# An xLSTM-style attention and two feed-forward layers on one core: queries and keys split in place instead of by a trip through DRAM, and a new order of work

## The chip, the cores and the metric

The kernel runs as one program on 1 core of a Trainium2 chip. The metric is the device time of one execution in microseconds (us), as a median of several runs; lower is better. Engines are named as in the profile: PE is TensorE (PEld its weight loads), DVE is VectorE, ACT is ScalarE, POOL is GpSimd, SP is SyncE, which issues all DMAs of this kernel, one after the other.

## The reference

Three layers follow each other. The attention is a recurrence over 768 steps for 4 batches of 8 heads with a head size of 40:

```
m_new  = maximum(f_gate[t] + m, i_gate[t])
f_stab = exp(f_gate[t] + m - m_new)
i_stab = exp(i_gate[t] - m_new);  m = m_new
C = f_stab * C + i_stab * outer(v[t], k[t])
n = f_stab * n + i_stab * k[t]
y[t] = sigmoid(o_gate[t]) * (C @ q[t]) / maximum(abs(n . q[t]), 1)
```

Its output, as 3072 rows of 320, goes through `maximum(maximum(x @ w1, x @ w2), x @ w3) @ w_out` (320 to 768 to 320; FFN1 below) and then through `h = x @ w_in; g = h * clip(h + 3, 0, 6) / 6; g @ w_out` (320 to 2048 to 320; FFN2 below). All weights are handed over as float64.

## The kernel before

The attention is cut into chunks of 128 steps. A group g is one batch in one chunk, so there are 24 groups, g = 4 * chunk + batch; `attention(g)` adds all steps of one. In a group, `scan` (L502) builds the decay matrix `fd` of each head on DVE, `sc` (L530) multiplies keys by queries on PE, `p` (L538) multiplies the scores by the decays, `inter` (L558) multiplies queries by the state of the chunk before, `pv` (L600) multiplies by the values, `rr`, `y0` and `y1` normalize, `tr` and `x` (L653, L658) transpose the result into `x1`, the input of FFN1, and `dc`, `cn` (L681, L700) carry the state on.

A product that has to keep nearly float32 accuracy is made of products in float32r: a number is split into a rounded high part and the remaining low part, and high*high, low*high and high*low are summed. For groups 8 to 23 (`GF = 8`) the three stand below each other on 120 rows of one tile: `qs` [120, 2, 8, 128] holds queries (index 0) and keys (index 1), and rows 0-39, 40-79 and 80-119 hold such parts that one product over 120 rows sums all three. Groups 0 to 7 use plain float32.

How `qs` of a group comes about, before: `lq` (L427) loads queries and keys as [128, 640] (`raw`), `sq` (L453, ACT) rounds them into the high part, `sl` (L457, POOL) subtracts for the low part, `sw` (L463) writes both parts to `qs_d` in DRAM (640 KB), and `sr` (L468) reads them back in five DMAs into the rows where they are wanted (960 KB):

```
nc.sync.dma_start(q[0:D], d[0].rearrange("a d n -> d a n"))
for r, (zq, zk) in enumerate(((0, 1), (1, 0)), 1):
    nc.sync.dma_start(q[r * D:r * D + D, 0], d[zq, 0])
    nc.sync.dma_start(q[r * D:r * D + D, 1], d[zk, 1])
```

The state of a group is spread over 120 rows (`cs`) in the same way: `ch` (L707, ACT) rounds, `cl` (L711, POOL) subtracts, `cd` (L716) moves the parts with six DMAs.

Weights are converted from float64 by steps on three engines, 24 pieces for FFN1 (`weights`, L732) and 32 for FFN2 (`w2_prep`, L939): a load (`load_f64`, L246, tile `raw`, four buffers), two conversions on ACT (`rebase` L251, `tail` L259), a join on DVE (L266), a rounding on ACT and a subtraction on POOL or DVE (`split`, L273). ACT reads a piece from its buffer, so a load can only go out when ACT is done with the piece four loads earlier.

FFN1 runs over blocks of 2, 2, 4, 4, 4, 4 and 4 groups (`BLK1`) and 6 pieces of 128 hidden columns: `f_in` (L773) makes three times eight matmuls into PSUM tile `h` (two buffers), whose first result is copied by ACT (`m`, L785) and the others joined by DVE (L787); `hh` (ACT, L797) and `hl` (POOL, L801) split the maximum, `f_out` (L806) multiplies it by the output weights into `acc`. `xd` (L850) writes the result to DRAM, two DMAs for each group; `x_load` (L952) reads it back for FFN2, which runs over 6 blocks of 512 rows and 16 pieces (`g_in` L971, `g_out` L991).

The order of the attention and of FFN1 on every engine is fixed before the program is built: each step is added with an engine, an assumed cost in ns, a priority (`pr`), the tiles it reads and writes; `Plan.order` (L143) plays them through with these costs and the buffer counts of `BUFS`, always takes the step that can start first (by priority where several can), and the instructions are written out in that order. `MOVED` (L42) adds a number to the priority of single steps. Priorities are 1000 * g plus an offset in `attention`, `WP0 + WPR * n` for the weights; `AHEAD` (L37) is how many groups ahead a group's queries may be loaded, `GP` and `NSG` place the gates of the chunks 1 to 5. FFN2 is ordered by the framework's own scheduler, which also puts its first weight loads and conversions among the steps of the attention. An engine works through its instructions strictly in the order written, SP as well: where one waits, all behind it wait.

Of the kernel before, what the change touches and what calls it, by code (L numbers as in the profile page):

```python
# [36 lines left out]
AHEAD, WP0, WPR = 5, 500, 100  # L37
GP, NSG = 1900, 4
GPB, GGB = 3, 4
PE_, PM, PC = 0, 2 * 10**6, 3 * 10**6  # L40

MOVED = {  # L42
    135: -1449, 206: -3641, 217: -1367, 319: 149, 371: 268, 387: 4201, 480: 39, 517: 2678, 522: 1135,
    539: 1040, 553: -4154, 559: -4352, 565: -156, 594: 613, 659: -1758, 707: -7, 715: 420, 742: -3344,
    940: 2702, 941: 5996, 953: 4436,
# [1035 lines left out]
```

## Time and profile before

| | |
|---|---|
| median of 3 runs | 793.09 us (789.65 to 795.54) |
| the profiled execution: time | 792.57 us |
| its span | 790.8 us |
| mean granted PE clock | 0.956 of full |
| PE busy | 757.2 us (96%), 5063 matmuls |
| DVE busy | 400.6 us (51%), 618 instructions |
| ACT busy | 309.2 us (39%), 597 instructions |
| POOL busy | 423.3 us (54%), 388 instructions |
| DMA, share of 16 engines | 38.2%, 91.82 MB |

The profile shows one execution; its span runs from the first to the last instruction, and 1.8 us of the time lie outside of it. Busy shares are means over a program with different stages: attention and FFN1 together in the first 380 us or so, the rest of FFN1 until 440 us, FFN2 until the end. The clock of PE is granted at one of two levels, 2.4 GHz (1.00 in the rows) or 1.2 GHz (0.50); a mean between them says how much of a stretch was spent at each.

### The profile page before, as it was taken

Reading aid. Unit: us, or ns where it says so; the run is one execution under the profiler, and the core shown is the slowest. Engines: PE = TensorE matmul, PEld = TensorE weight load, DVE = VectorE, ACT = ScalarE, POOL = GpSimd, SP = SyncE. Lnnn points to the kernel's source line nnn. Section 1 sums busy time; section 2 is a strip of 40 time slices with the busy share of each in tenths; the row PEclk is TensorE's granted clock in tenths of the full one; section 3 lists DMA queues with packets and bytes.
Section 4 is the critical chain, followed back from the end, with each engine's and each line's share of the span. In section 5 each row is a group of like instructions: output and inputs, shape, how many; then the busy total and the mean of one; then the engine's idle time right before and its main releaser. Section 6 shows DMA issues by size and latency. Waiting matters only on the chain.

```text
span 790.8 us, 13152 instructions
## 1 busy us (share of the span) xinstructions
PE 757.2 (96%) x5063; PEld 661.8 (84%) x5063; DVE 400.6 (51%) x618; ACT 309.2 (39%) x597; POOL 423.3 (54%) x388
## 2 busy tenths in 40 slices
PE   8878969899999998999999999999999999999997
PEld 6768869788888787888888878898998899898986
DVE  5987738668868776578425665312212113121210
ACT  4585422222223122222415886634433334433432
POOL 3788737757768687573514456535334334333331
PEclk7689679999999999999999999999999999999999
DMA  8578567675657758743322642200100000000000
GB/s 260 164 242 273 162 170 200 161 239 178 199 175 212 228 158 246 233 148 84 112 59 76 202 157 72 68 1 10 59 1 0 34 1 1 34 1 1 34 1 34
DMA packets 52078, 92.65 MB, mean 117 GB/s; under 512 B 6032, under 2 KB 28528, under 8 KB 52016
## 3 DMA queue, kind: packets, MB, share of 16 engines
q1 hardware_dynamic: 52016, 91.82, 38.2%
q8 instruction: 40, 0.66, 0.3%
q14 instruction: 22, 0.18, 0.1%
HBM read 70.78 MB, written 18.43 MB: 113 GB/s over the span
## 4 chain that ended last, share of the span: by engine, by line
PE 60%; DMA 11%; ACT 5%; DVE 4%; POOL 4%; SPq 3%; issue 2%; POOLq 0%; ACTq 0%; DVEq 0%
PE pi L284 20%; PE h L284 13%; PE po L1003 6%; PE po L1002 6%; PE po L1004 6%; DMA qs<-qs_d 4%; PE acc L817 3%; DMA raw<-in_w 2%; DMA qs_d<-sp 2%; SPq L720 2%; DVE t L267 2%; PE sc L536 1%; DMA fd<-f_d 1%; ACT a L255 1%; PE acc L819 1%
## 5 line engine op out<-in xcount | busy, mean ns | idle before, releaser
L284 PE MATMUL h<-x,w 128*128 128x512 f32 (+1 forms) x1008 | 224.8, 374 | 6.7 <-ACT m L785 6.7
L988 POOL TENSOR_TENSOR gg<-r,gg 128x512 fp32r<-128x512 f32 x96 | 125.6, 1318 | 184.4 <-ACT gg L987 174.3
L284 PEld LDWEIGHTS h<-x,w 128*128 128x128 f32 x1008 | 175.7, 198 | 36.3 <-ACT m L785 8.1
L284 PE MATMUL pi<-xs,w 128*128 128x512 f32 x768 | 193.0, 395 | 1.5 <-ACT w L946 0.8
L985 DVE SCALAR_TENSOR_TENSOR r<-r,pi 128x512 f32<-128x512 f32 x96 | 64.3, 686 | 230.3 <-ACT r L984 230.1
L284 PEld LDWEIGHTS pi<-xs,w 128*128 128x128 f32 x768 | 140.8, 188 | 29.7 <-ACT w L946 1.1
L1002 PE MATMUL po<-w,gg 128*128 128x320 f32 x384 | 118.3, 310 | 1.1 <-ACT gg L987 0.5
L1003 PE MATMUL po<-w,gg 128*128 128x320 f32 x384 | 118.0, 309 | 0.0
L984 ACT ACTIVATE r<-pi,b 128x512 f32<-128x512 f32 x96 | 64.0, 687 | 133.8 <-PE pi L284 133.2
L1004 PE MATMUL po<-w,gg 128*128 128x320 f32 x384 | 111.2, 309 | 0.0
L801 POOL TENSOR_TENSOR hh<-m,hh 128x512 fp32r<-128x512 f32 (+1 forms) x42 | 51.1, 1216 | 70.2 <-ACT hh L797 68.9
L787 DVE TENSOR_TENSOR m<-h,m 128x512 f32<-128x512 f32 (+1 forms) x84 | 50.9, 606 | 63.6 <-PE h L284 51.2
L1002 PEld LDWEIGHTS po<-w,gg 128*128 128x128 f32 x384 | 72.1, 188 | 5.7 <-ACT gg L987 1.5
L817 PE MATMUL acc<-hh,w 128*128 128x512 f32 (+1 forms) x252 | 76.5, 382 | 0.0
L1003 PEld LDWEIGHTS po<-w,gg 128*128 128x128 f32 x384 | 72.1, 188 | 3.0
L987 ACT CAST gg<-r 128x512 fp32r<-128x512 f32 x96 | 59.0, 621 | 36.6 <-DVE r L985 34.4
L797 ACT CAST hh<-m 128x512 fp32r<-128x512 f32 (+1 forms) x42 | 23.5, 559 | 125.7 <-PE acc L817 117.2
L1004 PEld LDWEIGHTS po<-w,gg 128*128 128x128 f32 x384 | 70.4, 188 | 1.0 <-POOL gg L988 0.2
L274 POOL TENSOR_TENSOR w<-t,w 128x384 fp32r<-128x384 f32 (+2 forms) x46 | 49.0, 1073 | 22.0 <-ACT w L946 11.5
L506 DVE TENSOR_TENSOR_SCAN fd<-fd,ident 128x512 f32<-128x512 f32 x40 | 58.1, 1462 | 2.5 <-DMA fd<-f_d 2.5
L267 DVE SCALAR_TENSOR_TENSOR t<-a,t 128x384 uint32<-128x384 uint32 (+1 forms) x56 | 46.0, 840 | 15.6 <-ACT t L263 14.0
L817 PEld LDWEIGHTS acc<-hh,w 128*128 128x128 f32 x252 | 47.0, 200 | 6.3
(107 smaller groups left out, 971.9 us busy)
## 6 DMA issues: line engine op xcount, KB each, us to landing
raw<-in_w SPq DMA_DIRECT2D x34, 384.0 KB
kvo<-in_kvo SPq DMA_DIRECT2D x22, 488.0 KB
fd<-f_d SPq DMA_DIRECT2D x20, 512.0 KB
qs_d<-sp SPq DMA_DIRECT2D x16, 640.0 KB
qs<-qs_d SPq DMA_DIRECT2D x64, 160.0 KB
raw<-in_w SPq DMA_DIRECT2D x22, 320.0 KB
raw<-in_qkf SPq DMA_DIRECT2D x16, 320.0 KB
qs<-qs_d SPq DMA_DIRECT2D x16, 320.0 KB
```

The source lines that it names most:

```text
L267: nc.vector.scalar_tensor_tensor(out=t, in0=a.bitcast(U32), scalar=3, in1=t, op0=ALU.logical_shift_left, op1=ALU.bitwise_or)
L284: nc.tensor.matmul(ps, wt[:, a:a + 128], x[:, r], start=n == 0, stop=n == len(order) - 1)
L506: nc.vector.tensor_tensor_scan(out=half, data0=s.get(("bc", a), half), data1=ident4.rearrange("p h t -> p (h t)"), initial=0.0, op0=ALU.mu ...
L801: nc.gpsimd.tensor_tensor(out=t[:, 1], in0=T["m", j, k], in1=t[:, 0].bitcast(F32), op=ALU.subtract)
L817: nc.tensor.matmul(acc[a], wo[:, a * 128:128 + a * 128], h, start=first, stop=last)
L984: nc.scalar.activation(r, ps, AF.Relu, bias=b3)
L985: nc.vector.scalar_tensor_tensor(out=r, in0=r, scalar=6.0, in1=ps, op0=ALU.min, op1=ALU.mult)
L987: nc.scalar.copy(gg[:, 0], r)
L988: nc.gpsimd.tensor_tensor(out=gg[:, 1], in0=r, in1=gg[:, 0].bitcast(F32), op=ALU.subtract)
L1002: nc.tensor.matmul(po[t], hi, wo[:, 0:320], start=first, stop=False)
L1003: nc.tensor.matmul(po[t], hi, wo[:, 320:640], start=False, stop=False)
L1004: nc.tensor.matmul(po[t], lo, wo[:, 0:320], start=False, stop=last)
```

## The change

Queries and keys of the groups 8 to 23 are loaded three times from the input as float32, each time into 40 of 120 rows of a tile `raw`, queries (a = 0) and keys (a = 1) apart. A constant `lows` [120, 2] is 1 on the rows where the low part is wanted and 0 elsewhere. `hm` on ACT writes float32r(lows * raw) into `sp`, `ls` subtracts it from `raw` into `qs`: on rows with 0 that leaves the rounded number itself, on rows with 1 the low part. Both run in halves of four heads (z), `ls` on DVE for the queries and on POOL for the keys. The DRAM tiles `qs_d` and the steps `sq`, `sl`, `sw`, `sr` are gone.

```diff
-                    s["raw"] = sb("raw", g, [128, QF])
-                    nc.sync.dma_start(s["raw"], qkf[g - GF])
+                    s["raw", a] = q = sb("raw", f"{g}_{a}", [120, H, L])
+                    for r in range(3):
+                        nc.sync.dma_start(q[r * D:r * D + D].rearrange("p h t -> p (h t)"), qkf[g - GF, :, a])
...
+                def hm(a, z):
+                    s["sp", a, z] = sb("sp", f"{g}_{a}{z}", [120, 4, L], F32R)
+                    x = s["raw", a][:, 4 * z:4 * z + 4]
+                    nc.scalar.activation(s["sp", a, z], x, AF.Copy, scale=lows[:, a:a + 1])
+
+                def ls(a, z):
...
+                    eng = nc.gpsimd if a else nc.vector
+                    eng.tensor_tensor(out=s["qs"][:, a, x], in0=s["raw", a][:, x], in1=s["sp", a, z].bitcast(F32), op=ALU.subtract)
...
-                P.add("ACT", 760, pr - 3000, sq, r=[("raw", g)], w=[("sp", g)])
-                P.add("POOL", 2000, pr - 3000, sl, r=[("raw", g)], w=[("sp", g)])
-                P.add("SP", 60, pr - 3000, sw, r=[("sp", g)], w=[("qd", g)], size=8 * 128 * QF)
-                P.add("SP", 300, pr - 2500, sr, r=[("qd", g)], w=[QS], size=120 * 8192)
```

The state goes to its 120 rows differently: `ch` on ACT makes three roundings of half a state each, one of them straight to other rows; `cl` on POOL writes the low part straight into rows 0-39 of `cs`, in two halves; two DMAs instead of six copy the high part to rows 40-119.

```diff
-                for n, x in enumerate(("cl", "ch", "ch")):
-                    for r in range(2):
-                        nc.sync.dma_start(
-                            t[n * D:n * D + D, 4 * r:4 * r + 4].bitcast(F32), s[x][64 * r:64 * r + D].bitcast(F32)
-                        )
+                for r in (D, 2 * D):
+                    nc.sync.dma_start(cs()[r:r + D].bitcast(F32), s["ch"][0:D].bitcast(F32))
```

The tiles `x2_d` between FFN1 and FFN2 are one for each block of FFN2, so `xd` and `x_load` need two DMAs for a block instead of two for a group. The planner's numbers change too: buffers, costs of SP's steps (60 ns becomes 360 for a DMA), the assumed latency of a DMA, a few constants, and the table of moved priorities, which grows from 21 entries to 175. New source lines shift by about 16 (L248 is L264 after, L255 L271, L263 L279, L720 L736).

```diff
-AHEAD, WP0, WPR = 5, 500, 100
-GP, NSG = 1900, 4
+AHEAD, WP0, WPR = 6, 500, 100
+GP, NSG = 1055, 4
...
+WLP, QLP = 800, 4000
...
-    135: -1449, 206: -3641, 217: -1367, 319: 149, 371: 268, 387: 4201, 480: 39, 517: 2678, 522: 1135,
...
+    21: -933, 44: 4396, 52: -6654, 63: -799, 66: 12937, 73: -3105, 74: 2861, 88: 693, 95: -1749,
...
-    qs=2, raw=1, sp=1, kvo=2, kvg=2, fd=2, vt=2, vw=2, nm=2, rr=2, y=2, sg=2, ct=1, cn=B + 1, ch=1, cl=1, cs=B + 1,
+    qs=2, raw=2, sp=1, kvo=2, kvg=2, fd=2, vt=2, vw=2, nm=2, rr=2, y=2, sg=2, ct=1, cn=B, ch=1, cs=B,
...
-                end = dma + 2000
+                end = dma + 2500
```

Two places of the new order matter below. The first is SP around the first weight loads of FFN2 (`raw2_k_p` is piece k, part p of FFN2's weights, `raw1_5_3` the last of FFN1's, the digit after another name is the group). Before:

```order
L248 DMA raw2_0_1_5219<-in_w2 128x320
L720 DMA cs5_1139<-cl5_1131 40x168 x2
L720 DMA cs5_1139<-ch5_1113 40x168 x4
L498 DMA fd7_1162<-f0_d_72 128x1024
L438 DMA kvo8_1196<-in_kvo 128x976
L471 DMA qs8_1218<-qs_d8_73 40x2x1024
L473 DMA qs8_1218<-qs_d8_73 40x1024
L474 DMA qs8_1218<-qs_d8_73 40x1024
L473 DMA qs8_1218<-qs_d8_73 40x1024
L474 DMA qs8_1218<-qs_d8_73 40x1024
L248 DMA raw2_1_0_5244<-in_w2 128x384
L248 DMA raw2_1_1_5254<-in_w2 128x320
```

and after:

```order
L264 DMA raw1_5_3_969<-in_w1 128x320
L506 DMA fd6_982<-f0_d_72 128x1024
L456 DMA kvo6_1015<-in_kvo 128x976
L264 DMA raw2_0_0_5268<-in_w2 128x384
L264 DMA raw2_0_1_5278<-in_w2 128x320
L456 DMA kvo8_1120<-in_kvo 128x976
L264 DMA raw2_1_0_5303<-in_w2 128x384
L264 DMA raw2_1_1_5313<-in_w2 128x320
L447 DMA qs7_1145<-in_qk0 40x1024 x2
L736 DMA cs5_1132<-ch5_1127 40x336 x2
```

Before, nine rows of SP stand between `raw2_0_1` and `raw2_1_0`, among them six DMAs of the state and five reads of `qs`; after, only the load of `kvo8` does, and the state comes behind the weights. ACT has the conversions of these pieces (`a2_1_0`) in its order at about the same place. Before:

```order
L263 ACTIVATE t2_0_1_5223<-raw2_0_1_5219 128x320
L255 ACTIVATE a2_1_0_5246<-raw2_1_0_5244 128x384
L255 ACTIVATE a2_1_1_5256<-raw2_1_1_5254 128x320
L797 CAST hh1_0_1288<-m1_0_1133 128x256
L785 COPY m0_5_1303<-h0_5_0_1279 128x256
```

The second place is ACT among the groups 10 to 12, where the roundings `hm` (L474) are new. After:

```order
L474 ACTIVATE sp10_01_1825<-raw10_0_1591,lows_90 120x512
L474 ACTIVATE sp10_11_1844<-raw10_1_1637,lows_90 120x512
L474 ACTIVATE sp10_10_1875<-raw10_1_1637,lows_90 120x512
L813 CAST hh1_5_1900<-m1_5_1676 128x256
L474 ACTIVATE sp12_11_1907<-raw12_1_1846,lows_90 120x512
L801 COPY m2_1_1915<-h2_1_0_1889 128x512
L670 CAST x13_1929<-tr8_1910 128x3x128
L474 ACTIVATE sp11_01_1961<-raw11_0_1902,lows_90 120x512
L474 ACTIVATE sp11_00_2016<-raw11_0_1902,lows_90 120x512
L813 CAST hh2_0_2059<-m2_0_1810 128x512
```

Before, ACT has one row `sp` for a whole group; after there are four, often one right behind the other, in front of the copies `m` and `hh` of FFN1 on the same engine.

## Rows read from the trace of the kernel before

**Rows 1.** Busy time by stretch: us, each engine busy (count), PEclk, DMA share, GB/s

```profile
20.00:40.00 20.00, 17.37 (x108) 14.88 (x108) 18.09 (x28) 11.81 (x25) 14.48 (x15) 0.61 0.55 164
40.00:60.00 20.00, 15.27 (x137) 13.63 (x136) 16.88 (x30) 17.00 (x43) 16.43 (x19) 0.83 0.75 240
60.00:80.00 20.00, 17.28 (x168) 16.06 (x164) 15.02 (x28) 9.87 (x24) 16.53 (x19) 0.91 0.81 271
80.00:100.00 20.00, 18.22 (x144) 17.64 (x141) 14.49 (x26) 8.20 (x20) 15.06 (x16) 0.67 0.58 163
100.00:120.00 20.00, 13.89 (x108) 13.21 (x107) 7.58 (x16) 4.18 (x10) 7.59 (x9) 0.73 0.58 159
120.00:140.00 20.00, 20.00 (x205) 19.77 (x205) 15.29 (x30) 5.47 (x14) 15.14 (x17) 0.91 0.77 219
140.00:160.00 20.00, 17.94 (x171) 15.60 (x170) 14.95 (x24) 4.17 (x9) 14.76 (x16) 0.96 0.62 158
...
180.00:260.00 80.00, 80.00 (x679) 67.41 (x678) 63.27 (x98) 20.50 (x39) 60.43 (x59) 1.00 0.60 185
...
300.00:340.00 40.00, 37.45 (x281) 31.03 (x280) 23.72 (x39) 10.10 (x19) 23.56 (x23) 1.00 0.77 237
...
380.00:440.00 60.00, 60.00 (x268) 49.37 (x266) 28.30 (x35) 26.34 (x51) 22.98 (x17) 1.00 0.33 92
440.00:500.00 60.00, 57.45 (x306) 49.71 (x305) 36.04 (x51) 47.45 (x101) 33.11 (x27) 1.00 0.40 131
500.00:780.00 280.00, 280.00 (x1551) 252.11 (x1550) 60.45 (x83) 110.50 (x182) 110.02 (x82) 1.00 0.05 17
```

**Rows 2.** Timeline of ACT, 84 to 114 us: start, us, instruction [idle before, releaser]

```profile
105.91 0.54 ACT L255 ACTIVATE a<-raw 128x384 f32<-128x384 f32 x1 [12.27 <-DMA raw<-in_w]
```

**Rows 3.** Timeline of PE, 96 to 112 us

```profile
107.83 2.08 PE L284 MATMUL h<-x,w 128*128 128x256 f32 x8 [6.11 <-ACT m L785]
```

**Rows 4.** Timeline of SP, 70 to 108 us: time of issue, us to issue

```profile
85.45 1.54 SPq L720 DMA_DIRECT2D cs<-cl  x2
87.04 3.87 SPq L720 DMA_DIRECT2D cs<-ch  x4
91.03 0.41 SPq L498 DMA_DIRECT2D fd<-f_d  x1
91.55 0.36 SPq L438 DMA_DIRECT2D kvo<-in_kvo  x1
...
94.05 5.50 SPq L248 DMA_DIRECT2D raw<-in_w  x4
```

**Rows 5.** Waits of PE, whole span: who for what, us, times, longest

```profile
PE sc L536 <- DMA cs<-ch: 2.2, 1, 2.2
PE sc L536 <- DMA qs<-qs_d: 2.1, 1, 2.1
```

**Rows 6.** Groups by line and form: count, busy us, mean ns, idle before

```profile
L458 POOL TENSOR_TENSOR sp<-raw,sp 128x640 fp32r<-128x640 f32 x16 | 29.1, 1822 | 7.1 <-ACT sp L455 7.0
...
L593 DVE TENSOR_TENSOR pr<-fd 128x512 f32<-128x512 f32 x32 | 26.4, 838 | 0.5
...
L598 POOL TENSOR_TENSOR pr<-pr 128x512 bf16<-128x512 f32 x16 | 21.3, 1334 | 16.9 <-DVE pr L593 16.3 <-DMA x_d<-x 0.6
...
L797 ACT CAST hh<-m 128x512 fp32r<-128x512 f32 x30 | 18.6, 621 | 104.3 <-PE acc L817 98.8 <-DVE rr L637 5.5
...
L455 ACT CAST sp<-raw 128x640 fp32r<-128x640 f32 x16 | 11.7, 730 | 1.2 <-DMA qs_d<-sp 1.2
...
L713 POOL TENSOR_TENSOR cl<-cn,ch 128x168 fp32r<-128x168 f32 x16 | 10.9, 680 | 1.1 <-ACT ch L709 1.1
...
L709 ACT CAST ch<-cn 128x168 fp32r<-128x168 f32 x16 | 5.3, 332 | 10.0 <-DMA cs<-ch 5.7 <-DVE cn L705 4.3
```

**Rows 7.** One line's instructions (L593): ns min/median/max, first and last start

```profile
L593 DVE TENSOR_TENSOR pr<-fd x32: 674/693/1809, 126.1 to 367.9; 128x512 f32<-128x512 f32 x32
```

**Rows 8.** Busy time in the stretch with the split groups, columns as in rows 1

```profile
145.00:380.00 235.00, 229.72 (x1906) 192.34 (x1905) 173.09 (x268) 55.73 (x105) 160.19 (x153) 0.99 0.63 187
```

More of the change, by code (lines that the diff above doesn't have):

```diff
@@ L26 @@
 DM = H * D
-QF = 2 * D * H * L // 128
 FF1, FF2 = 768, 2048
@@ L236, in body @@
     f0_d = dram.tile([NC_ - 1, BH, L], F32, name="f0_d")
-    qs_d = [dram.tile([2, 2, D, H * L], F32, name=f"qs_d{g}") for g in range(GF, G)]
-    x2_d = [dram.tile([128, 3, L], F32, name=f"x2_d{g}") for g in range(G)]
+    x2_d = [dram.tile([128, 3, n * L], F32, name=f"x2_d{j}") for j, n in enumerate(BLK2)]
     def prio(p):
@@ L422, in attention, with lq @@
             per_head = lambda x: x.unsqueeze(2).to_broadcast([128, H, DP])
-            QS, FD, KVO = ("qs", g), [("fd", g, a) for a in range(2)], ("kvg" if g < 2 else "kvo", g)
-            def lq():
+            QS, FD, KVO = [("qs", g, a, z) for z in range(2) for a in range(2)], [("fd", g, a) for a in range(2)], ("kvg" if g < 2 else "kvo", g)
+            def lq(a=0):
                 if g < GF:
@@ new lines, in ls @@
+                def ls(a, z):
+                    if "qs" not in s:
+                        s["qs"] = sb("qs", g, [120, 2, H, L], F32R)
+                    x = slice(4 * z, 4 * z + 4)
+                    eng = nc.gpsimd if a else nc.vector
+                    eng.tensor_tensor(out=s["qs"][:, a, x], in0=s["raw", a][:, x], in1=s["sp", a, z].bitcast(F32), op=ALU.subtract)
+                for z in range(2):
+                    for a in range(2):
+                        SPL, Q = ("sp", (g, a, z)), ("qs", g, a, z)
+                        P.add("ACT", 600, pr - QLP + 1000 + z, lambda a=a, z=z: hm(a, z), r=[("raw", (g, a)), ("lows",)], w=[SPL])
+                        P.add("POOL" if a else "DVE", 1220 if a else 600, pr - QLP + 1000 + z, lambda a=a, z=z: ls(a, z), r=[("raw", (g, a)), SPL], w=[Q])
@@ L576, in attention @@
                 nr = 2 if g < GF else 1
-                IN, ST = [("pa", f"in{g}_{r}") for r in range(nr)], ("cs" if g >= GF else "cn", g - B)
-                P.add("PE", 990, pr + 25, inter, r=[QS, ST], w=IN, wait=300)
+                IN, ST = [("pa", f"in{g}_{r}") for r in range(nr)], [("cs", g - B, r) for r in range(3)] if g >= GF else [("cn", g - B)]
+                P.add("PE", 990, pr + 25, inter, r=[*(QS if g < GF else QS[0:4:2]), *ST], w=IN, wait=300)
                 for r in range(nr):
@@ L726, in attention @@
                 return
-            P.add("ACT", 280, pr + 70, ch, r=[("cn", g)], w=[("ch", g)])
-            P.add("POOL", 580, pr + 71, cl, r=[("cn", g), ("ch", g)], w=[("cl", g)])
-            P.add("SP", 300, pr + 72, cd, r=[("ch", g), ("cl", g)], w=[("cs", g)], size=4 * 120 * 336)
+            for r in range(2):
+                P.add("ACT", 280 + 280 * r, pr + 70, lambda r=r: ch(r), r=[("cn", g)], w=[("ch", g, r)])
+            for r in range(2):
+                P.add("POOL", 520, pr + 71, lambda r=r: cl(r), r=[("cn", g), ("ch", g, r)], w=[("cs", g, r)])
+            P.add("SP", 1420, pr + 72, cd, r=[("ch", g, 0), ("ch", g, 1)], w=[("cs", g, 2)], size=4 * 80 * 336)
         def weights(k, p):
@@ L888, in owns, with low_rows @@
             nc.vector.tensor_reduce(side, x.rearrange("p b r h -> p r b h"), axis=mybir.AxisListType.XY, op=ALU.add)
+        def low_rows():
+            for a, x in enumerate((2 * D, D)):
+                nc.vector.tensor_reduce(lows[:, a:a + 1], ident[0:120, x:x + D], axis=mybir.AxisListType.X, op=ALU.add)
+        P.add("DVE", 300, 3000, low_rows, r=[("id",)], w=[("lows",)])
         P.add("POOL", 300, -1500, owns, r=[("id",)], w=[("own",)])
```

89 lines of the change are left out of this document (39 added, 50 removed), and 19 rows, old and new, of the table MOVED.

## The prediction

> **What bounds the kernel now.** I read busy time by stretch first, then the waits of PE, then the timelines around the longest of them. From 500 to 780 us PE is busy 280.00 of 280.00 us at full clock, and from 380 to 440 us 60.00 of 60.00 [rows 1]: those stages are bound by PE, and the change leaves their products alone. What can be won is the time in which PE stands or runs at 1.2 GHz, and nearly all of it lies before 120 us. From 20 to 120 us PE is idle 2.63, 4.73, 2.72, 1.78 and 6.11 us of the five stretches of 20, 18.0 us in all. Their clocks, 0.61, 0.83, 0.91, 0.67 and 0.73, mean 2 x (1 - clock) x 20 = 15.6, 6.8, 3.6, 13.2 and 10.8 us at the lower level, 50.0 us, of which PE was busy about 82%, so that about half of 41 us, 20 us, went to the clock. Later there is little: 2.06 us idle at 140 to 160, 2.55 at 300 to 340, 2.55 at 440 to 500 [rows 1]; these add to 7.2 us.
>
> The longest single wait of PE is 6.11 us at 107.83, for ACT's copy `m` [rows 3]. ACT itself had stood 12.27 us until 105.91, for a piece of FFN2's weights [rows 2]. SP says why that piece was late. Its load was issued in the row at 94.05, behind the DMAs of the state that wait from 85.45 on and end at 90.91 (87.04 + 3.87), a load of `fd`, one of `kvo`, and the reads of `qs` [rows 4]; it landed 11.9 us later. PE's clock is 0.67 and 0.73 around this [rows 1], since it stood.
>
> DVE is the engine next to the limit: 18.09 of 20 us from 20 to 40, and 173.09 of 235 us, 74%, in the stretch in which the split groups run (145 to 380); POOL has 160.19 there, 68%, ACT 55.73, 24% [rows 1, 8].
>
> **The change part by part.** The sum is made against the profiled execution, 792.6 us, which is 0.5 us under the median of the three runs, 793.1.
>
> (1) The late weights. In the new order the pieces raw2_1_0 and raw2_1_1 stand right behind raw2_0_1 and one load of `kvo`, ahead of the state, so SP need not wait for the state before it issues them; what remains is the wait for their buffers, two pieces of FFN1's weights that ACT reads some ten rows earlier. If the load of `kvo8` (488 KB), raw2_0_0, raw2_0_1 (384 and 320 KB) and itself (384 KB) all stood behind each other, 1.61 MB at the 271 GB/s of the stretch from 60 to 80 us [rows 1] take 5.9 us in place of 11.9, and ACT still has work for most of that. The stretch from 80 to 120 us lost 7.89 us idle and, with 24.0 us at the lower clock and PE busy 80% of it, about 9.6 us to the clock. I count the 6.1 us of the wait in full and half of the clock's loss: -10.9. The bounds are -3 (another wait of PE takes most of the place: the transposes of the groups 4 to 7 come right behind) and -17.5 (all that the stretch lost).
>
> (2) No trip by DRAM. Per group `sw` and `sr` move 640 and 960 KB and `lq` 320; after, six loads move 960 KB: half, 15.7 MB less over 16 groups. SP issues 13 DMAs for queries and state now, eight later. Those of the state take 0.77 and 0.97 us each in the rows (1.54 over two, 3.87 over four), plain loads 0.36 to 0.41 [rows 4]: about 2.6 + 5.4 us a group now, about 2.3 + 1.9 later, 3.8 us less. SP is not on PE's path as such; what counts is that `qs` and `cs` come in time. PE waited once for each, 2.1 and 2.2 us [rows 5], and these are the 2.06 and most of the 2.55 us of idle time at 140 to 160 and 300 to 340 [rows 1]. I count -4, with bounds 0 (the loads come as late by a buffer) and -4.6.
>
> (3) The order in the ramp, 20 to 80 us. The steps there are the same, none is taken away, and FFN1's first products are moved ahead of the scores of group 3. DVE is busy 50.0 of 60 us, DMA has shares of 0.55 to 0.81 [rows 1]. Where the engines that feed PE are busy to this degree, a new order finds little: -2. PE lost 10.1 us idle there and, by 26.0 us at the lower clock and 83% busy, 10.8 us to the clock; I bound the gain by a good third of it, -8, and the loss by the same argument from below, +4.
>
> (4) The added work beside PE. DVE gets 32 subtractions of [120, 512]. The nearest row is `pr` (L593), also a float32 subtraction of 512 with both inputs in SBUF: 838 ns in the mean [rows 6], so +26.8 us. POOL loses 16 x 1822 ns and gets 32 x 1334 (L598), and for the state gets 32 in place of 16 subtractions of 680: +24.4. ACT loses 16 x 730 ns and gets 64 roundings, each at most the 621 of `hh` (L797), and for the state 48 in place of 16 of 332: +38.7 [rows 6]. If all of it fell into the 235 us of rows 8, DVE would come to 199.9 us, 85%, POOL to 79%, ACT to 40%. All this lies beside PE, which has FFN1's products to do in between, so it costs nothing directly; it costs where a step comes late in PE's fixed order. The copies `m` and `hh` are behind the roundings on ACT, and a rounding waits until the subtraction in front has freed `sp`, which has one buffer: 1.3 us on POOL if it starts at once. PE's first results of FFN1 wait behind that in one of two `h` buffers. I take +3, with bounds 0 and +14 (below).
>
> A gain from DVE I exclude, as no work leaves it. Here the Trainium skill speaks against the change: its page "SBUF — State Buffer", section "Who interferes with whom", says that a DVE instruction with two SBUF inputs contends with a POOL instruction that reads SBUF, and that the later one waits for the whole of the other. The trace agrees that such instructions stretch: the median of L593 is 693 ns, its maximum 1809 [rows 7].
>
> (5) The rest. `x2_d` in blocks saves SP issues around 135 to 450 us; FFN2's first input is read while PE has FFN1 to do (60.00 of 60.00 us busy from 380 to 440), so 0. Buffers of `cn` and `cs` go from five to four: the state of a group is read by the group four later, whose own state comes after that, so 0. The conversion of FFN2's weights, on which PE loses 2.55 us from 440 to 500 [rows 1], stays the same work: 0, with +2 and -2 as bounds.
>
> Sum: -10.9 - 4 - 2 + 3 = -13.9, so 792.6 - 13.9 = 778.7, forecast 779 us. With the terms near their ends I get a range of its own for this case of 770 to 786.
>
> **Rivals.** *The gain is taken up elsewhere* (about 790). The ramp is fed by DVE at 83% and DMA at up to 0.81; taking one wait of ACT away then only lets PE run into the next one. For it speaks that PE was idle 10.1 us from 20 to 80 us without any single wait as long as the one at 107.83; against it, that DVE and POOL are busy only 7.58 and 7.59 of 20 us from 100 to 120, so that they too stood behind ACT [rows 1]. Term (1) at -3, (2) at -2, (4) at +3 and (3) at 0: 790.6.
>
> *The ramp gets shorter throughout* (about 765). The round trips of the first split groups weigh on the same DMA engines as the weights at 75 to 81% share, and the new table of moved steps removes small waits as well. (1) at -17.5, (2) at -4.6, (3) at -6, (4) at 0: -28, 764.5. Against it speaks that DVE's work in the ramp stays the same.
>
> *DVE becomes the bound* (slower, about 806). If each of the 32 subtractions on DVE took the 1809 ns of the longest L593 [rows 7], DVE would need 173.1 + 57.9 = 231 of 235 us. From 20 to 40 us it was busy 90%, and PE was idle 2.63 of 20 us, 13% [rows 1]; 13% of 235 us are 31 us, less -17 of (1), (2) and (3), so +14: 806. It decides from DVE busy 90% on, a mean of (211.5 - 173.1) / 32 = 1.2 us for a subtraction. Against it: medians of 693, and FFN1 lags behind the attention by some 60 us, which evens out delays. The rule of the Trainium skill named above is the mechanism of this rival: by full exclusion the subtractions would be near the long end.
>
> **How the numbers follow.** A run of this kernel can tell a difference of about 1%, 8 us, from none. Forecast 0.50, shorter ramp 0.20, gain taken up 0.22, DVE the bound 0.08. Faster by over 1% (under 785): nearly all of the forecast (0.47), all of the shorter ramp and 0.03 of the gain taken up, 0.70. Slower by over 1% (over 801): 0.07 of DVE the bound. The rest, 0.23, is within 1%. The range reaches from the case of the shorter ramp, 763, to a little over that of the gain taken up, 793; it leaves out DVE the bound and the edge of the shorter ramp.
>
> **What would show it.** Right: ACT's wait for a weight piece near 95 us is under 4 us; the clock from 80 to 120 us is above 0.8; no wait of PE for `qs`; queue bytes near 76 MB; L481 on DVE under 1 us in the mean; the start of FFN1's block of groups 4 to 7 some 10 us earlier; 500 us to the end unchanged in length. Wrong: PE waits for `m` or `sc` of 2 us and more between 150 and 380 us, DVE busy over 90% there, or ACT standing in front of L474 with `m` and `hh` behind it; then the cost of (4) was sized wrongly. If the ramp's clock stays at 0.7 with no long wait, (1) and (3) were.

## The result and the profile after

The change makes the kernel slower by 0.7%: 798.63 us in the median of 20 runs (793.91 to 803.25) against 793.25 us (786.64 to 803.29) of the kernel before on the same chip, ratio 1.0071 with a 95% interval of 1.0047 to 1.0095. Forecast were 779 us, 763 to 793. All ratios here and below leave out those executions of before that are more than 1.5% above its fastest one; before ran beside every experiment on the same chip. The profiled execution of after took 794.38 us, its span is 792.7 us (before 790.8).

The first look goes to a mark of progress that both traces have: the copy of one FFN1 accumulator (`x2`, block `j`, seven times). Its row gives the first and the last start; the columns are duration in ns (min/median/max), then first and last start in us. Before:

```profile
L848 DVE COPY x<-acc x7: 424/691/692, 132.5 to 441.3; 128x512 f32<-128x512 f32 x5, 128x256 f32<-128x256 f32 x2
```

After:

```profile
L864 DVE COPY x<-acc x7: 414/684/692, 116.3 to 444.4; 128x512 f32<-128x512 f32 x5, 128x256 f32<-128x256 f32 x2
```

The first block is done 16.2 us earlier, the last one 3.1 us later. From the first to the last it takes 328.1 us in place of 308.8, 19.3 more; from the last to the end of the span 348.3 in place of 349.5. So -16.2 + 19.3 - 1.2 = +1.9 us, the difference of the spans. By this mark a gain came in the ramp, and more than all of it was given back while the split groups run. Each trace is one execution, and the mark varies: in the runs below that are made from after, the first copy starts between 112.0 us (e6) and 120.5 us (e10), and in e12, which only adds work to before, at 128.4 us. So some 4 us of such a figure can be the single trace's.

Busy time by stretch of after, columns as in [rows 1]:

```profile
80.00:100.00 20.00, 17.34 (x176) 15.94 (x174) 19.06 (x32) 13.66 (x33) 17.86 (x21) 1.00 0.71 223
100.00:120.00 20.00, 19.98 (x176) 19.15 (x175) 15.20 (x31) 7.82 (x18) 15.30 (x18) 0.83 0.41 129
...
145.00:380.00 235.00, 221.93 (x1842) 182.20 (x1841) 199.08 (x289) 87.70 (x162) 187.85 (x173) 0.99 0.38 121
180.00:260.00 80.00, 73.27 (x635) 60.14 (x634) 72.28 (x103) 32.46 (x61) 70.01 (x66) 1.00 0.44 138
...
380.00:440.00 60.00, 57.74 (x250) 46.45 (x249) 23.99 (x28) 22.90 (x43) 22.71 (x16) 1.00 0.29 89
...
500.00:780.00 280.00, 280.00 (x1547) 251.74 (x1545) 61.45 (x81) 110.34 (x182) 112.11 (x83) 1.00 0.05 17
```

From 80 to 120 us the clock is 1.00 and 0.83 (before 0.67 and 0.73, [rows 1]) and PE is idle 2.7 us in place of 7.9. From 145 to 380 us DVE has 199.1 us and POOL 187.9 us, as the forecast worked out (85% and 79%); but PE is idle 13.1 us in place of the 5.3 of [rows 8], and between 180 and 260 us, where it had been busy throughout, 6.7 us. From the first to the last copy PE is idle 17.5 us (before 5.3), 12.2 of the 19.3 us; in the other 7.1 the profile counts it as busy with nearly the same products, which was not looked into. FFN2 from 500 us on is the same.

On SP the late weights stand where the order said; the columns are those of [rows 4]:

```profile
82.23 1.39 SPq L264 DMA_DIRECT2D raw<-in_w  x2
83.67 0.73 SPq L447 DMA_DIRECT2D qs<-in_qk  x2
84.50 1.63 SPq L736 DMA_DIRECT2D cs<-ch  x2
```

The two of the first row are raw2_1_0 and raw2_1_1, issued 11.8 us earlier than in [rows 4] and ahead of the state. The stall of ACT of 12.27 us [rows 2] and PE's wait of 6.11 us behind it [rows 3] are gone. One difference in the ramp is not named above: until 36 us PE runs 34 products `wps` of a constant tile, whose result no step reads, where before runs 16 (13.0 us in place of 6.9). They fill idle time that the planner foresees on PE; what they do to the clock or the time was not tried.

PE's longest waits in after:

```profile
PE sc L544 <- POOL qs L481: 7.1, 5, 2.0
PE tr L664 <- POOL y L655: 4.3, 5, 1.2
PE h L300 <- ACT m L801: 4.2, 6, 1.1
```

The waits for `cs` and for `qs` from DRAM [rows 5] have gone; in their place PE waits for the subtraction of the keys on POOL, for `y` on POOL, and for the copy `m` on ACT. The groups of instructions by line and form, as in [rows 6]:

```profile
L514 DVE TENSOR_TENSOR_SCAN fd<-fd,ident 128x512 f32<-128x512 f32 x40 | 66.1, 1661 | 2.2 <-DMA fd<-f_d 2.2
L481 POOL TENSOR_TENSOR qs<-raw,sp 120x512 fp32r<-120x512 f32 x32 | 49.1, 1534 | 12.9 <-ACT sp L474 10.9 <-issue 1.4
L474 ACT ACTIVATE sp<-raw,lows 120x512 fp32r<-120x512 f32 x64 | 46.3, 724 | 62.7 <-POOL qs L481 35.2 <-DVE qs L481 18.8 <-DMA raw<-in_qkf 7.7
L601 DVE TENSOR_TENSOR pr<-fd 128x512 f32<-128x512 f32 x32 | 32.5, 1019 | 2.3 <-PE pv L618 1.7
L481 DVE TENSOR_TENSOR qs<-raw,sp 120x512 fp32r<-120x512 f32 x32 | 29.2, 913 | 7.2 <-ACT sp L474 7.1
L730 POOL TENSOR_TENSOR cs<-cn,ch 40x168 fp32r<-40x168 f32 x32 | 25.8, 807 | 3.4 <-ACT ch L721 2.1
```

New are 49.1 us of subtractions on POOL, 29.2 on DVE and 46.3 of roundings on ACT, in front of which ACT stood 35.2 + 18.8 = 54 us for the one buffer of `sp`. Old operations are longer: `pr` (L601; 838 ns in [rows 6]) takes 1019 ns.

What PE waits for in the steady part is seen in the chain of waits, here of 203 to 213 us (start, us, what):

```profile
203.75 1.16 POOL qs L481
204.91 0.09 issue
205.00 1.48 POOL cs L730
206.48 0.07 issue
206.55 0.89 POOL cs L730
207.44 0.07 issue
207.51 0.48 POOL ct L704
207.98 0.71 POOL vr L592
208.70 0.07 issue
208.77 0.75 POOL vr L595
209.52 1.25 POOL hh L817
210.77 2.19 POOL qs L481
```

From 203.75 us on POOL runs through its queue with no gap above 0.09 us, and a subtraction of keys stands at the end of this row. The PE timeline has the answer to it, one of the five waits of 7.1 us in all:

```profile
213.01 0.66 PE L544 MATMUL sc<-qs 120*128 120x128 f32 x4 [1.99 <-POOL qs L481]
```

### The profile page after: what moved, and what is told of

Read it like the earlier page. It is cut to its first block, busy times and chain, and to the rows that moved or that the text cites. A ratio compares the mean times of both kernels' runs of the same rounds, so it can differ in the third digit from the quotient of the medians.

```text
span 792.7 us, 13185 instructions
## 1 busy us (share of the span) xinstructions
PE 758.5 (96%) x5081; PEld 653.8 (82%) x5081; DVE 437.4 (55%) x652; ACT 353.3 (45%) x677; POOL 462.4 (58%) x420
## 3 DMA queue, kind: packets, MB, share of 16 engines
q1 hardware_dynamic: 28592, 75.22, 30.1%
## 4 chain that ended last, share of the span: by engine, by line
PE 59%; DVE 13%; POOL 12%; ACT 7%; issue 5%; DMA 3%; SPq 0%; POOLq 0%; DVEq 0%; ACTq 0%
PE pi L300 20%; PE h L300 12%; PE po L1025 6%; PE po L1024 6%; PE po L1026 6%; POOL qs L481 3%; PE acc L833 3%; DVE fd L514 2%; DVE t L283 2%; POOL hh L817 2%; DVE qs L481 2%; POOL cs L730 1%; ACT a L271 1%; PE sc L544 1%; POOL y L655 1%
## 5 line engine op out<-in xcount | busy, mean ns | idle before, releaser
L1010 POOL TENSOR_TENSOR gg<-r,gg 128x512 fp32r<-128x512 f32 x96 | 125.7, 1318 | 183.2 <-ACT gg L1009 173.1
L300 PE MATMUL h<-x,w 128*128 128x512 f32 (+1 forms) x1008 | 227.2, 374 | 5.4 <-ACT m L801 4.2
L300 PEld LDWEIGHTS h<-x,w 128*128 128x128 f32 x1008 | 172.7, 195 | 36.3 <-ACT m L801 6.3
L817 POOL TENSOR_TENSOR hh<-m,hh 128x512 fp32r<-128x512 f32 (+1 forms) x42 | 56.6, 1347 | 39.1 <-ACT hh L813 39.0
L474 ACT ACTIVATE sp<-raw,lows 120x512 fp32r<-120x512 f32 x64 | 46.3, 724 | 62.7 <-POOL qs L481 35.2
L833 PE MATMUL acc<-hh,w 128*128 128x512 f32 (+1 forms) x252 | 74.1, 374 | 0.0
L514 DVE TENSOR_TENSOR_SCAN fd<-fd,ident 128x512 f32<-128x512 f32 x40 | 66.1, 1661 | 2.2 <-DMA fd<-f_d 2.2
L290 POOL TENSOR_TENSOR w<-t,w 128x384 fp32r<-128x384 f32 (+2 forms) x46 | 46.3, 1015 | 26.8 <-ACT w L768 16.8
L481 POOL TENSOR_TENSOR qs<-raw,sp 120x512 fp32r<-120x512 f32 x32 | 49.1, 1534 | 12.9 <-ACT sp L474 10.9
```

Of the source, the lines that this page charges most:

```text
L300: nc.tensor.matmul(ps, wt[:, a:a + 128], x[:, r], start=n == 0, stop=n == len(order) - 1)
L481: eng.tensor_tensor(out=s["qs"][:, a, x], in0=s["raw", a][:, x], in1=s["sp", a, z].bitcast(F32), op=ALU.subtract)
L514: nc.vector.tensor_tensor_scan(out=half, data0=s.get(("bc", a), half), data1=ident4.rearrange("p h t -> p (h t)"), initial=0.0, op0=ALU.mu ...
L817: nc.gpsimd.tensor_tensor(out=t[:, 1], in0=T["m", j, k], in1=t[:, 0].bitcast(F32), op=ALU.subtract)
L833: nc.tensor.matmul(acc[a], wo[:, a * 128:128 + a * 128], h, start=first, stop=last)
L1010: nc.gpsimd.tensor_tensor(out=gg[:, 1], in0=r, in1=gg[:, 0].bitcast(F32), op=ALU.subtract)
```

## The experiments

Three theories were to be told apart. "Work": the subtractions make steps late in PE's fixed order. "Buffer": ACT stands in front of L474 for the one buffer of `sp`, and `m` and `hh` stand behind it. "Order": the new order itself costs the steady stretch. The runs e2, e3, e5 and e6 leave out most of a subtraction from group 10 on, so they serve for measuring only. The table gives for each run the ratio to before, the busy time from 145 to 380 us and the time from the first to the last copy of an FFN1 accumulator, read as above. The ratio is of many executions, the two columns behind it are of one: those of e1 and e13 come from slow ends of their twelve (799.97 and 799.49 us, medians 795.32 and 793.36).

| run | ratio, 95% interval | PE / DVE / ACT / POOL busy of 235 us | first to last block, us |
|---|---|---|---|
| before | 1 | 229.7 / 173.1 / 55.7 / 160.2 | 308.8 |
| after | 1.0071 (1.0047-1.0095) | 221.9 / 199.1 / 87.7 / 187.9 | 328.1 |
| e1, three buffers | 1.0041 (1.0009-1.0072) | 221.3 / 203.4 / 85.9 / 190.5 | 330.3 |
| e2, no subtraction | 0.9831 (0.9779-0.9882) | 230.1 / 177.1 / 92.1 / 158.2 | 311.7 |
| e3, none on POOL | 0.9848 (0.9801-0.9896) | 229.8 / 192.6 / 92.6 / 162.5 | 314.6 |
| e4, trip from group 12 | 0.9947 (0.9909-0.9985) | 225.3 / 183.8 / 66.8 / 173.3 | 321.1 |
| e5, POOL fills instead | 0.9987 (0.9957-1.0018) | 224.9 / 196.9 / 88.4 / 188.0 | 323.4 |
| e6, none on DVE | 0.9973 (0.9943-1.0003) | 225.9 / 181.8 / 90.4 / 182.8 | 325.6 |
| e7, state's on DVE | 1.0042 (1.0015-1.0070) | 222.9 / 207.2 / 87.6 / 174.9 | 327.4 |
| e8, keys' on DVE | 0.9944 (0.9913-0.9975) | 225.7 / 210.7 / 91.5 / 155.0 | 323.0 |
| e9, before, early weights | 0.9930 (0.9890-0.9971) | 228.7 / 167.1 / 58.2 / 154.9 | 310.0 |
| e10, e8 and three buffers | 0.9950 (0.9920-0.9981) | 226.6 / 211.9 / 87.4 / 156.8 | 321.6 |
| e11, e10 and `v` on ACT | 0.9951 (0.9914-0.9988) | 226.1 / 207.6 / 111.2 / 141.0 | 322.1 |
| e12, before, added work | 1.0088 (1.0053-1.0123) | 221.0 / 202.2 / 53.5 / 179.0 | 319.6 |
| e13, e1, `v` and `y` on ACT | 0.9978 (0.9945-1.0011) | 221.6 / 197.0 / 134.7 / 162.8 | 329.2 |
| e14, e4 and `v` on ACT | 0.9982 (0.9947-1.0017) | 223.0 / 178.4 / 91.8 / 160.6 | 325.3 |

**e1, more buffers for `sp`.**

```diff
-s["sp", a, z] = sb("sp", f"{g}_{a}{z}", [120, 4, L], F32R)
+if a and "sp2" in late:
+    s["sp", a, z] = late["sp2"].tile([120, 4, L], F32R, tag="sp2", name=f"sp{g}_{a}{z}", bufs=2)
+else:
+    s["sp", a, z] = sb("sp", f"{g}_{a}{z}", [120, 4, L], F32R)
...
+late["sp2"] = c1.enter_context(pool("sp2p", side="right"))
```

> The changed kernel, but the subtractions of POOL take their rounded halves from two buffers of their own instead of sharing the one of `sp` with DVE; the order on every engine stays. Theory "work" (the 32 subtractions on DVE, 29 us, and the 32 on POOL, 49 us, fill DVE to 85% and POOL to 80% from 145 to 380 us, and steps come late in PE's fixed order): ACT's 54 us of waits in front of L474 shrink to under 25 us, but the time stays, ratio to the kernel before 1.004 to 1.009. Theory "buffer" (ACT stands behind `sp`, and `m` and `hh` behind ACT): most of the 15.7 us that PE lost more than before from 140 to 400 us come back, ratio 0.988 to 0.995. Theory "order" (the new order itself costs the steady stretch): ratio 1.005 to 1.009.

ACT's row shows the wait gone:

```profile
L477 ACT ACTIVATE sp<-raw,lows 120x512 fp32r<-120x512 f32 x64 | 45.1, 721 | 24.2 <-DVE qs L484 12.3 <-DMA raw<-in_qkf 9.8 <-POOL qs L484 1.7
```

62.7 us have become 24.2, and POOL's 35.2 of them 1.7; but PE is busy 221.3 of the 235 us, as in after. The ratio is 1.0041, its interval overlaps that of after. So the buffer is not the main cause; by the ratios it is 0.3%, within the noise.

**e2 and e3, the subtractions cut.** (`e` is `8 if g >= GF + 2 else L` in e2, the same for POOL's half alone, `a == 1`, in e3.)

```diff
-s["qs"] = sb("qs", g, [120, 2, H, L], F32R)
+s["qs"] = T[g - 2]["qs"] if g >= GF + 2 else sb("qs", g, [120, 2, H, L], F32R)
...
-eng.tensor_tensor(out=s["qs"][:, a, x], in0=s["raw", a][:, x], in1=s["sp", a, z].bitcast(F32), op=ALU.subtract)
+eng.tensor_tensor(out=s["qs"][:, a, x, 0:e], in0=s["raw", a][:, x, 0:e], in1=s["sp", a, z][:, :, 0:e].bitcast(F32), op=ALU.subtract)
```

> The changed kernel, but from group 10 on (counted from 0) each subtraction L481 takes 8 of 128 columns of each head only, on DVE and on POOL, into queries and keys that otherwise keep the values of groups 8 and 9, so the subtraction is left out by 15 sixteenths there. Roundings, loads, waits and order stay. Theory "work": some 20 us go from DVE and some 38 us from POOL between 145 and 380 us, the other DVE operations get shorter (L601 back from a median of 1030 to about 700 ns), ratio 0.980 to 0.990. Theory "buffer": the same range, as `sp` comes free at once; the run with more buffers tells these two apart. Theory "order": 1.002 to 1.008.

> As the run with both subtractions cut, but only those on POOL are cut to 8 of 128 columns from group 10 on; DVE's are whole. Theory "work" with POOL as the engine that comes late (PE's longest remaining wait for this part was sc behind POOL's qs, 7.1 us): ratio within 0.004 of the run with both cut. With DVE as the engine: no more than a third of what both give, ratio 0.997 to 1.004. Theory "buffer": 35 of ACT's 54 us of waits were for POOL, so about two thirds of the gain, 0.990 to 0.996. Theory "order": 1.004 to 1.008.

Without the subtractions from group 10 on the changed kernel takes 779.36 us, without POOL's alone 781.14 us. "Order" falls: this is the new order, with its loads, roundings and waits, and it is 1.5 to 1.7% faster than before. Of e3, busy time from 145 to 380 us:

```profile
145.00:380.00 235.00, 229.84 (x1891) 191.33 (x1892) 192.59 (x294) 92.57 (x170) 162.52 (x176) 0.99 0.41 129
```

PE has its busy time of [rows 8] again, with DVE still at 193 us. POOL's subtractions, of which 28 of 32 are cut here, are most of the price: 1.0071 - 0.9848 = 2.2%.

**e4, the trip for the later groups.** The groups 8 to 11 have the new form, 12 to 23 the old one.

```diff
+if g >= TRIP:
...
+    P.add("ACT", 760, pr - QLP + 1000, sq, r=[RAW], w=[SP_])
...
+    P.add("POOL", 2000, pr - QLP + 1000, sl, r=[RAW], w=[SP_])
+    P.add("SP", 400, pr - QLP + 1000, sw, r=[SP_], w=[("qd", g)], size=8 * 128 * QF)
+    P.add("SP", 1800, pr - QLP + 1500, sr, r=[("qd", g)], w=QS, size=120 * 8192)
```

> The changed kernel, but groups 12 to 23 (counted from 0) split their queries and keys as before, by one rounding on ACT, one subtraction of 128x640 on POOL and the trip through DRAM; groups 8 to 11 and everything up to about 120 us stay in the new form. Groups 12 to 19 keep their moved steps, groups 20 to 23 have none. Theory "work" or "buffer": the 12.7 us that PE is ahead by at 140 us are kept except for what the plan without moved steps costs, ratio 0.983 to 0.993. Theory "order": 1.000 to 1.008.

0.9947: faster than both kernels, less than expected. Between 130 and 400 us PE waits 5.8 us for `m` on ACT here, in after 2.9; the plan for this mixture, with no moved steps in its last four groups, is one that nobody tuned, so this run bounds little.

**e5, POOL's time without its reads.** As e3, and behind each cut subtraction on POOL:

```diff
+nc.gpsimd.memset(late["scr"], 0.0)
```

> As the run with POOL's subtractions cut to 8 of 128 columns, but POOL fills a scratch tile of 120x1240 with zeros behind each of them, some 1.1 us, so that POOL is as long busy as with the whole subtraction and reads nothing for it. Theory "POOL's time" (POOL at 80% hands its results over late): ratio 1.000 to 1.009, PE busy about 222 us from 145 to 380. Theory "contention" (the reads of POOL's subtractions stretch DVE's operations, and DVE is late): ratio 0.983 to 0.990, PE busy about 230 us there.

POOL is as long busy as in after, and reads nothing for it:

```profile
145.00:380.00 235.00, 224.91 (x1864) 185.73 (x1863) 196.93 (x294) 88.38 (x164) 187.95 (x202) 0.99 0.39 123
```

0.9987 lies between the two theories. From e3 to e5 it is 0.9987 - 0.9848 = 1.4%: POOL's time alone, which makes what stands behind it late. From e5 to after it is 0.8%: here the subtraction itself comes later, and POOL reads two tiles; the two were not told apart. In e5 the scans of DVE took 1526 ns, in e3 1471, in after 1661.

**e6, DVE's half cut.** As e3, with `not a`.

> The other half of the cut: only DVE's subtractions L481 are cut to 8 of 128 columns from group 10 on, POOL's are whole. Theory "POOL's time": little comes back, ratio 0.999 to 1.006. Theory that DVE and POOL cost alike, so that any 15 to 25 us less beside PE pay: 0.984 to 0.992.

0.9973, 1.0% under after and under the range for POOL as the only cause, 0.999 to 1.006. But the parts do not add: DVE's cut gives 1.0%, POOL's 2.2%, both 2.4%. Why is not shown: a rounding that waits for the subtraction before it, on DVE and POOL in turn, would make them pieces of one path, but e1 takes most of that wait away and gains 0.3%.

**e7, the state's subtractions on DVE.**

```diff
-nc.gpsimd.tensor_tensor(
+nc.vector.tensor_tensor(
     out=cs()[0:D, x], in0=s["cn"][64 * r:64 * r + D], in1=s["ch"][64 * r:64 * r + D, x].bitcast(F32), op=ALU.subtract
```

> The changed kernel with the 32 subtractions of the state, L730, on DVE in place of POOL; all else stays, the order too. POOL loses 25.8 us, DVE gains 32 times about 320 ns, 10 us (by L713, 128x168). Theory "POOL's time": POOL falls from 188 to about 164 of 235 us, as in the run with POOL's cut, so ratio 0.984 to 0.993, with DVE at 88%. Theory "DVE is the bound" (decides near 90%): ratio 1.005 to 1.015.

A miss, 1.0042. The operation was mis-sized:

```profile
L730 DVE TENSOR_TENSOR cs<-cn,ch 40x168 fp32r<-40x168 f32 x32 | 20.0, 626 | 0.5
```

626 ns on DVE, not 320, for 807 saved on POOL. And POOL fell only to 174.9 us, because of the 32 operations of 25.8 us only 20 lie between 145 and 380 us in after (groups by line and form in that window):

```profile
L730 POOL TENSOR_TENSOR cs<-cn,ch 40x168 fp32r<-40x168 f32 x20 | 15.5, 775 | 2.5 <-ACT ch L721 1.6
```

So the run took 13 us of load from POOL, not the 25 of e3, and put 8 on DVE; it decides little.

**e8 and e10, the keys on DVE as well.** e10 adds the buffers of e1.

```diff
-eng = nc.gpsimd if a else nc.vector
+eng = nc.vector
```

> The changed kernel with all subtractions L481 on DVE, 64 in place of 32, none on POOL. POOL falls from 188 to about 140 of 235 us, DVE rises from 199 by 32 times 0.9 us to about 228, 97%, less what its other operations get shorter. Theory "POOL's time" alone: ratio 0.983 to 0.990. Theory "DVE is the bound" from 90% on, the mechanism of the slower rival: 1.005 to 1.020.

> The changed kernel with all subtractions L481 on DVE, as one run before, and those of the keys with two buffers of their own for the rounded halves, as another. In the first of these ACT still stood 49.6 us in front of L474 for DVE. If that wait holds back `m` and `hh`, ratio 0.986 to 0.992. If DVE at 90% is what is left, the same as with one buffer, 0.992 to 0.998.

Of e8, the stretch and the subtraction:

```profile
145.00:380.00 235.00, 225.66 (x1864) 186.06 (x1862) 210.67 (x316) 91.45 (x167) 154.95 (x147) 0.99 0.41 126
...
L481 DVE TENSOR_TENSOR qs<-raw,sp 120x512 fp32r<-120x512 f32 x64 | 53.1, 829 | 4.5 <-ACT sp L474 4.0
```

With DVE at 210.7 us, 90%, the kernel is faster than with DVE at 85% and POOL at 80%: 0.9944, and in e10 with DVE at 211.9 us 0.9950. So the slower rival, DVE as the bound from 90% on, is not what happened. A subtraction takes 829 ns where none runs on POOL, 913 in after. The waits for `sp` again do not matter (0.9950 with three buffers).

**e9, one part of the change alone.** The kernel before, with the weight pieces issued ahead of the state (`early` loads them):

```diff
 def cd():
+    if g == 5:
+        early((0, 1), (1, 0), (1, 1))
```

> The kernel before with one part of the change: the loads raw2_1_0 and raw2_1_1 stand on SP right behind raw2_0_1, ahead of the state and the queries of group 8; all else stays, but for a copy `ch6` on ACT that moves by four rows and the next two weight loads, which come later. If term (1) of the forecast is right, ACT's stall of 12.27 us near 95 us goes, the clock from 80 to 120 us rises, and the ratio is 0.983 to 0.990 (11 us). If another wait takes its place, 0.995 to 1.000. If the ramp gain of the changed kernel came from its other parts (no trip, new order), ACT's stall goes, but the ratio is 0.994 or more.

ACT's waits for weight loads in front of its conversions are 1.4 us in all. The first copy of an accumulator starts at 123.3 in place of 132.5 us, the last at 433.3 in place of 441.3; the busy time of the stretch in which PE had stood, and of the one before it:

```profile
80.00:100.00 20.00, 18.22 (x149) 17.38 (x149) 14.33 (x27) 9.56 (x22) 15.08 (x16) 0.67 0.48 149
100.00:120.00 20.00, 20.00 (x189) 19.35 (x189) 15.12 (x27) 5.28 (x13) 12.58 (x16) 0.95 0.87 251
```

PE was busy 13.89 us from 100 to 120 us [rows 1]. The ratio is 0.9930, between the ranges that were expected. So the early weights are worth 8 to 9 us in the trace, and they are kept: from block to block it takes 310.0 us, before 308.8. By the ratio it is 0.7%, 5.5 us, and by its interval 2.3 to 8.7. The clock from 80 to 100 us is 0.67 as before [rows 1], although the stall is gone.

**e11, e13 and e14, products moved from POOL to ACT.** `v` in all three, in e13 also the first product of `y`:

```diff
-nc.gpsimd.tensor_tensor(out=s["vt"], in0=s["v"], in1=per_head(isl), op=ALU.mult)
+for h in range(H):
+    nc.scalar.activation(s["vt"][:, h], s["v"][:, h], AF.Copy, scale=isl[:, h:h + 1])
```

> The run with all subtractions on DVE and three buffers, and in it the product `v` of the groups 8 to 23 on ACT, eight activations of 128x42 per group, in place of one operation of some 920 ns on POOL. Theory "sum" (over all runs so far what PE loses from 145 to 380 us goes with the busy time of DVE and POOL together: about 5 us at 333 to 355 us of it, 8 to 10 at 357 to 369, 10 to 14 at 382 to 394; not with one engine's share): the sum falls from 369 to about 354, PE loses some 5 in place of 8.4, ratio 0.988 to 0.992. Theory "DVE at 90% is the limit": no change, 0.994 to 0.997. If ACT, with eight more operations per group in front of `m` and `hh`, comes late: 0.997 or more.

> The changed kernel with two buffers of their own for the rounded halves of the keys, and with two products of the groups 8 to 23 moved from POOL to ACT: `v` (some 920 ns on POOL) and the first one of `y` (some 850 ns), each as eight activations with a scale per row. The subtractions stay on DVE and POOL as in the changed kernel. If POOL's load alone above about 165 of 235 us is the price (DVE at 193 to 199 us cost little where POOL had 162), POOL falls from 190 to about 163 and PE loses some 6 in place of 13.7 us there: ratio 0.985 to 0.991. If DVE at 199 us costs as much as it did at 208: 0.993 to 0.998. If ACT, which then has 140 of 235 us, comes late with `m` and `hh`: 1.000 or more.

> The run in which the groups 12 to 23 take the trip through DRAM again, with `v` of the groups 8 to 23 on ACT. DVE stays at about 184, POOL falls from 173 to about 160 of 235 us. If both engines under these loads cost nothing over the kernel before (5.3 us lost at 173 and 160), the ramp's gain is kept: ratio 0.982 to 0.990. If what that run lost (9.7 us, of it 5.8 us in waits for `m` on ACT) comes from its plan without moved steps and from ACT, no change or worse: 0.993 to 1.000.

e11 takes 16 us more from POOL and gains nothing (0.9951 against 0.9950), so "sum", by which PE's loss goes with the busy time of DVE and POOL together, falls there. e14, 0.9982, takes 13 us from the POOL of e4 and gains nothing either. e13 goes furthest: DVE 197.0 and POOL 162.8 us, nearly the loads of e3, but PE is busy 221.6 us in place of 229.8:

```profile
145.00:380.00 235.00, 221.60 (x1839) 182.16 (x1840) 196.99 (x290) 134.69 (x391) 162.78 (x146) 0.99 0.39 123
```

One of POOL's own waits in it, 130 to 400 us:

```profile
POOL y L666 <- ACT sg L661: 19.9, 10, 6.7
```

Eight activations take the place of one operation and POOL now waits for ACT. The load of POOL went, and PE lost as much as in after; that the group's steps still came late is the reading that fits, but it was not followed step by step.

**e12, the added work put into the kernel before.**

```diff
 def sl():
     nc.gpsimd.tensor_tensor(out=s["sp"][:, 1], in0=s["raw"], in1=s["sp"][:, 0].bitcast(F32), op=ALU.subtract)
+    for e in (nc.vector, nc.vector, nc.gpsimd):
+        if e in late:
+            e.tensor_tensor(out=late[e], in0=late[e], in1=late[e], op=ALU.subtract)
```

> The kernel before, unchanged but for added work that nobody waits for: behind each `sl` of the 16 split groups, two subtractions of 120x512 on DVE and one on POOL, each on a scratch tile of its own. This is what the change adds to the two engines between 145 and 380 us, some 26 and 24 us, with the order, the trip through DRAM and all else as before. Theory "sum": the sum rises from 333 to about 380, PE loses 10 to 12 in place of 5.3 there, ratio 1.005 to 1.011. Theory "order" (the work is hidden, the new order or the split's own waits cost the time): 0.998 to 1.003.

```profile
145.00:380.00 235.00, 221.01 (x1844) 183.08 (x1843) 202.22 (x286) 53.48 (x102) 179.01 (x161) 0.99 0.63 185
```

1.0088. With the old order, the old trip and work that no step waits for, PE loses 14.0 us in place of 5.3, and its blocks take 319.6 us in place of 308.8. DVE has 3 us more than in after (its subtractions took 1341 ns here), POOL 9 less. So work on DVE and POOL is not free here even where no step uses its result. It costs 0.9%, less than half of what the subtractions of after cost, where PE waits for the results too.

## Why the prediction was wrong

The ramp came out about as forecast in sum, but not term by term. Terms (1) and (3) have -12.9 us for it, and the first block of FFN1 is done 16.2 us earlier, give or take some 4. Term (1), -10.9, was sized too high: the early weights alone give 5.5 us by the ratio of e9, about the 6.11 us of PE's wait. Half of what the clock cost from 80 to 120 us was counted with it, as if the stall were its reason; but in e9, without the stall, the clock is still 0.67 from 80 to 100 us and only from 100 to 120 higher, 0.95. The rest of the ramp's gain is more than the -2 of term (3); how much of it is the order, how much the trip, and how much the added products `wps`, was not tried. Term (2), -4, lay at 140 to 160 and 300 to 340 us, behind the ramp. Its two waits are gone from PE's list, but no time was gained there that a trace shows: even without the subtractions (e2) PE is idle 4.9 us from 145 to 380 us, where before it was 5.3. The loads fell to 75.22 MB ("near 76").

Term (4) failed: "All this lies beside PE, which has FFN1's products to do in between, so it costs nothing directly", +3 us with bounds of 0 and +14. By the trace it is +19.3 us from the first to the last block, beyond its upper bound. By the runs, what the subtractions cost is 1.0071 - 0.9831 = 2.4% of 793 us, 19 us. That e2 takes 779.36 us, the time that was forecast, is in part luck: it leaves out nearly all of the subtractions, and terms (1) and (2) came out smaller than said. Each load was worked out rightly (DVE 85%, POOL 79%, ACT 40% said; 85, 80 and 37 found). Wrong was the step from load to time. PE's order is fixed, and from 145 to 380 us it holds for each group scores, products, transposes and state, each of which waits for a chain over ACT, DVE and POOL. With DVE at 74% and POOL at 68% [rows 8] PE was idle 5.3 us; with some 26 us more on each it is idle 13.1, of which 7.1 are waits for the keys on POOL. The chain at 203 to 213 us shows one of these as a row of eight POOL operations, the last of them the keys.

Single operations took longer than was reckoned: the roundings 724 ns where "at most the 621" was taken, the state's 807 on 40 partitions where before it had been 680 on 128, POOL's subtraction 1534 where 1334 was taken; DVE's, 913, was close. As the loads came out as said, this is not the step that failed. But the planner of after reckoned with still less: 600 ns for a rounding, 1220 and 600 for the subtraction on POOL and DVE, 520 for the state's. An order made with the measured times was not tried; it is the rival that is left, for the fixed order may be late because it was made for shorter steps.

The slower rival, DVE as the bound, had the side right, and 0.08 as its chance, but not the mechanism: DVE at 90% in e8 is faster than after, and POOL's half is worth more than DVE's (e3, e6). Two of the three signs named for "wrong" did come: PE waiting 2.0 us for `sc`, and ACT in front of L474 with `m` and `hh` behind it; DVE over 90% did not. Of these the second is nearly harmless by itself (e1). Most signs named for "right" came as well, as they look at the ramp, the bytes and FFN2, and not at what the stretch from 145 us on loses.

On contention: the median of `pr` rose from 693 [rows 7] to 1030 ns (L601):

```profile
L601 DVE TENSOR_TENSOR pr<-fd x32: 641/1030/1776, 120.0 to 366.1; 128x512 f32<-128x512 f32 x32
```

and the mean of the scan from 1462 ns in before to 1661 (L514 above):

```profile
L506 DVE TENSOR_TENSOR_SCAN fd<-fd,ident 128x512 f32<-128x512 f32 x40 | 58.1, 1462 | 2.5 <-DMA fd<-f_d 2.5
```

With POOL's subtractions cut the scan is at 1471, with POOL filling a tile instead at 1526. The Trainium skill, page "SBUF — State Buffer", section "Who interferes with whom", says that such DVE instructions contend with a POOL instruction that reads SBUF and not with one that only writes it; the direction agrees. As the whole cost it would not do: POOL's time without reads (e5 against e3) already makes 1.4 of the 2.2%.

What stays open: no single figure gives the cost of a load. e3 and e13 have nearly the same busy times on DVE and POOL and differ by 14.6 us from block to block in their traces and by 1.3% in their ratios; ACT has 134.7 us in e13 and 92.6 in e3. e14 has DVE and POOL near the loads of before, and still 325.3 us, with a plan that was not tuned for it. That lateness on the path of a group decides is argued from the waits; no run here sorted it by step.

The fastest version found with the whole computation is e9, the kernel before with only its weight loads put earlier: 0.9930, that is faster than before by 0.7% and than after by 1.4%. e4, e8, e10 and e11 are within its interval.

## What to carry to other kernels

Work on engines "beside" the bound one is not free because they have room left. Here DVE was at 74% and POOL at 68% under a fixed order; a like load put on the old kernel (e12) shows without any rewrite that more of it costs, though less than half of what it cost where PE waits for its results. Follow a mark of progress, such as the start of each block's copy, through the whole trace: a gain in one stage can be seen whole and be lost in the next. A split that triples the rows gives the engines three times the columns: 64 halves of 512 here, where before it was 16 tiles of 640. Fewer rows did not make up for it (120x512 took ACT 724 ns, 128x640 730), and half the DMA bytes for queries and keys did not pay for it.

## What the runs showed of the hardware

Small operations cost more than in proportion to their columns: a subtraction of 120x32 on POOL took 509 ns in e5, one of 120x512 1534 in after; an activation of 128x42 took 318 ns (e11), so eight of them 2.5 us where POOL does the same 128x336 in about 0.92. A subtraction on DVE whose inputs and output are one tile took 1341 ns for 120x512 (e12), the one with three tiles 913 in after. Why was not tried.
